# Projections of keys and queries: full rows in four matmuls against half rows in eight pairs

## Chip, cores and metric

The kernel runs on one core of one Trainium2 chip. The metric is the device time of one execution in microseconds; the time of a kernel is the median of its runs. The times before are 278.46, 279.36, 278.23 and 278.74 us, median 278.6 us.

## What is computed

The reference is a linear attention with an exponential feature map, followed by a gated MLP that mixes along the sequence. There are 8 batches, 8 heads, 576 tokens and head size 64; the feature map has 128 features, the MLP 512 inputs and 2 x 512 hidden units.

```
def phi(x):
    proj = einsum('bhsd,df->bhsf', x, w_phi)            # 64 -> 128
    proj = proj - max(abs(proj), axis=-1)
    return concatenate([exp(proj), exp(-proj)], axis=-1)
q_p, k_p = phi(q), phi(k)
kv = einsum('bhsf,bhsd->bhfd', k_p, v);  z = sum(k_p, axis=2)
x  = einsum('bhsf,bhfd->bhsd', q_p, kv) / (einsum('bhsf,bhf->bhs', q_p, z) + 1e-6)
h  = relu(x_as[b, s, 512] @ w_in);  u, v = halves of h
v_n = layernorm(v)
out = (u * (w_spatial @ v_n + b_spatial)) @ w_out
```

## The kernel before, in words

**Units.** The attention is cut into 36 units: 32 of them are pairs of heads of one batch over the first 512 tokens, and 4 are the last 64 tokens of two batches and all heads. A unit always has 8 blocks of 128 tokens by 64 features, which lie as `kT` and `qT`, tiles of 128 rows by 4 x 128 columns: in each column block j, rows 0 to 63 are one block and rows 64 to 127 are the next one. For the first two batches TensorE transposes them (`a_transpose`, L248 to L261); for later batches a DMA does (`cross`, L116). The units of the last tokens are always transposed by TensorE, with a copy of `kT` on ScalarE or VectorE and of `qT` on VectorE.

**Projection.** `by_token` (L263) multiplies one half of `kT` or `qT` by `wphi2`, which holds `w_phi` twice on a block diagonal (rows 0 to 63 by columns 0 to 127, rows 64 to 127 by columns 128 to 255, zeros elsewhere). So one matmul with 128 rows and 256 columns projects two blocks at once, half of the products being with zeros. Two such matmuls fill a PSUM bank with 4 blocks; keys take two banks per unit and queries two. For keys (`a_keys`, L270) VectorE takes the maximum of the absolute values over a bank (L278) and ScalarE takes the two exponentials from it (L281); `a_scale` then makes `em` on ScalarE (L301) and the scaled values `vs` on GpSimd (L306). For queries (`a_queries`, L283) VectorE takes the maxima (L292), and GpSimd (VectorE for the first five units) splits them into a bf16 high part and rest, `mhl` (L295, L296). Later steps turn `mhl` by a transpose on TensorE (L327), make the query features (L344 and L365, or L348 to L359), sum keys by values (`a_kv`, L378, L380), and multiply queries by these sums (`a_num`, L398, with reciprocal and product on VectorE, L388, L389).

**Filler.** The MLP of each batch is a list of tasks, mostly groups of 128x512 matmuls of 0.85 to 1.07 us: `b_v` (L447, then ScalarE L449 and VectorE L450, L451; its normalisation on GpSimd, L461 to L467, comes as a task of its own), `b_u` (L515, ScalarE L517), `b_s` (L536, VectorE L539), `b_o` (L561, then VectorE or ScalarE L564 in turn, and a DMA out). They wait in `queue` and are dealt out between the parts of the attention, by a credit in microseconds of matmul time:

```
ORDER = (("keys", 0.375), ("queries", 0.25), ("attention", 0), ("sums", 0.25),
         ("next", 0.125), ("features", 0), ("out", 0), ("maxima", 0))
...
    credit[0] = min(credit[0] + rate[0] * share, CAP)
    while queue and credit[0] >= queue[0][0] / 2:
        cost, task = queue.pop(0)
        task()
        credit[0] -= cost
```

`CAP` is 2.11, and `rate` is at most `MOST` = 4.0 per step (L622 to L637). `step(i)` (L648) runs the parts in the order of `ORDER`, each for the unit that is due by its lag, and calls `fill(share)` after each. What is left of the queue after the last step is run at the end (L737).

**What sets the order.** Each engine runs its instructions in a fixed order, that in which `step` builds them; the framework's scheduler moves only neighbours past each other, and not those under `pin`. So the order of `step` is that of TensorE, VectorE, ScalarE, GpSimd and the DMA queues. All PSUM tiles come from one pool of 8 banks (L57) that are given out in turn: a new tile waits until the tile eight before it has been read.

The profile names lines of this kernel. The first filler task stands in the step of unit 8, and the last projection is that of unit 35.

Of the kernel before, what the change touches and what calls it, by code (L numbers as in the profile page):

```python
# [8 lines left out]
FP32 = mybir.dt.float32  # L9
BF16 = mybir.dt.bfloat16  # L10
AF = mybir.ActivationFunctionType
ALU = mybir.AluOpType
AX = mybir.AxisListType
# [3 lines left out]
def kernel(  # L17
# [15 lines left out]
    nc = tc.nc  # L33

    B, H, S, D = q.shape
    F = w_phi.shape[1]
# [3 lines left out]
    P = 128  # L40
# [16 lines left out]
    psum = ctx.enter_context(tc.tile_pool(name="psum", bufs=8, space=bass.MemoryType.PSUM))  # L57
# [81 lines left out]
    bias = cpool.tile([P, NB], FP32)  # L139
# [8 lines left out]
    wphi2 = cpool.tile([P, 2 * F], BF16)  # L148
# [12 lines left out]
    for i in range(NM):  # L161
        for tiles, name in ((mhl, "mhl"), (mT, "mT")):
            t = cpool.tile([P, P], BF16, name=f"{name}{i}")
# [21 lines left out]
    for y in range(2):  # L185
        r = slice(y * D, (y + 1) * D)
# [7 lines left out]
    for i in range(2):  # L194
        pin(nc.scalar.copy)(out=alternate(wm, i),
                            in_=wphi2[:, i * F:(i + 1) * F].unsqueeze(1).to_broadcast([P, NP, F]))
# [51 lines left out]
    def a_transpose(u):  # L248
        if u["pair"] and u["b"] >= XB:
            return  # L250
        src = st[u["b"]] if u["pair"] else gs[u["g"]]
        for x, copy in (("k", nc.vector.tensor_copy if u["i"] < EK else nc.scalar.copy), ("q", nc.vector.tensor_copy)):
            pt = psum.tile([P, 4, P], BF16, tag="bank", name="pt")
            for j in range(4):
                if u["pair"]:
                    blk = src[x][u["pj"] // 2][:, 2 * (u["pj"] % 2) + j // 2, (j % 2) * P:(j % 2 + 1) * P]
                else:
                    blk = src[x][:, 2 * j:2 * j + 2, :]
                nc.tensor.transpose(out=pt[:, j, :], in_=blk, identity=ident)
            u[x + "T"] = a1.tile([P, 4, P], BF16, tag="kT", name="kT") if x == "k" else qts[u["i"] % len(qts)]  # L260
            copy(out=u[x + "T"], in_=pt)  # L261

    def by_token(xT, half):  # L263
        ps = psum.tile([P, 4, F], FP32, tag="bank", name="ps")
        for x in range(2):
            nc.tensor.matmul(out=ps[:, 2 * x:2 * x + 2, :], lhsT=xT[:, 2 * half + x, :], rhs=wphi2,  # L266
                             start=True, stop=True)
        return ps

    def a_keys(u):  # L270

        u["mk"] = small.tile([P, H], FP32, tag="mk", name="mk")
        u["kf"] = feat.tile([P, 2, H, F], BF16, tag="kf" if u["pair"] else "kf_t", name="kf",
                            bufs=4 if u["pair"] else 2)
        for half in range(2):
            pk = by_token(u["kT"], half)
            hs = slice(4 * half, 4 * half + 4)
            nc.vector.tensor_reduce(out=u["mk"][:, hs], in_=pk, axis=AX.X, op=ALU.max,  # L278
                                    apply_absolute_value=True)
            for s, sc in ((0, 1.0), (1, -1.0)):  # L280
                nc.scalar.activation(out=u["kf"][:, s, hs, :], in_=pk, func=AF.Exp, bias=0.0, scale=sc)  # L281

    def a_queries(u):  # L283

        m, early = mhl[u["i"] % NM], u["i"] < EARLY
        if not early:
            mq = small.tile([P, H], FP32, tag="mq", name="mq")
        for half in range(2):
            pq = by_token(u["qT"], half)
            if early and half == 0:  # L290
                mq = pq[:, 0, 0:H]
            nc.vector.tensor_reduce(out=mq[:, 4 * half:4 * half + 4], in_=pq, axis=AX.X, op=ALU.max,  # L292
                                    apply_absolute_value=True)
        eng = nc.vector if early else nc.gpsimd
        eng.tensor_copy(out=m[:, 0:H], in_=mq)  # L295
        eng.tensor_tensor(out=m[:, H:2 * H], in0=mq, in1=m[:, 0:H], op=ALU.subtract)  # L296

    def a_scale(u):
        em = small.tile([P, 2, H], FP32, tag="em" if u["pair"] else "em_t", name="em", bufs=3 if u["pair"] else 1)
        for s, sc in ((0, -1.0), (1, 1.0)):  # L300
            nc.scalar.activation(out=em[:, s, :], in_=u["mk"], func=AF.Exp, bias=0.0, scale=sc)  # L301
        if u["pair"]:
            pj = u["pj"]
            vs = feat.tile([P, 2, H, DA], BF16, tag="vs", name="vs", bufs=4)
            for s in range(2):
                nc.gpsimd.tensor_tensor(out=vs[:, s, :, 0:D], in0=st[u["b"]]["v"][:, pj * H:(pj + 1) * H, :],  # L306
                                        in1=em[:, s, :].unsqueeze(2).to_broadcast([P, H, D]), op=ALU.mult)
            nc.gpsimd.tensor_copy(out=vs[:, :, :, D:DA], in_=em.unsqueeze(3).to_broadcast([P, 2, H, 2]))
            u["vs"] = vs
        else:  # L310
            d = gs[u["g"]]
            d["vs"], d["unit"], d["em"] = vst[u["g"] % 2], u, em
            for bl in range(2 if u["g"] else 1):
                tail_scale(u["g"], bl)
# [10 lines left out]
    def a_max_t(u):  # L325
        pt = psum.tile([P, P], BF16, tag="bank", name="pt")
        nc.tensor.transpose(out=pt, in_=mhl[u["i"] % NM], identity=ident)  # L327
        if merged(u):
            odd, even = u["qT"][0:2 * H], u["qE"][D:D + 2 * H]
            nc.vector.tensor_copy(out=odd, in_=pt[0:2 * H, :].unsqueeze(1).to_broadcast([2 * H, 4, P]))  # L330
            nc.vector.tensor_copy(out=even, in_=pt[0:2 * H, :].unsqueeze(1).to_broadcast([2 * H, 4, P]))
            return
        nc.vector.tensor_copy(out=mT[u["i"] % NM][0:2 * H, :], in_=pt[0:2 * H, :])
# [34 lines left out]
    def a_kv(u):  # L368
        d, dg, bl = st[u["b"]], gs[u["g"]], u["b"] % 2
        if u["pj"] == 0:  # L370
            d["kv"] = feat.tile([P, H, 2, DA], BF16, tag="kv", name="kv", bufs=3)
        ut = dg["unit"]
        pv = psum.tile([P, 2, 2, DA], FP32, tag="bank", name="pv")
        for hh in range(2):
            h = 2 * u["pj"] + hh
            for s in range(2):
                for c in range(NB):
                    nc.tensor.matmul(out=pv[:, hh, s, :], lhsT=u["kf"][:, s, 4 * hh + c, :],  # L378
                                     rhs=u["vs"][:, s, 4 * hh + c, :], start=(c == 0), stop=False)
                nc.tensor.matmul(out=pv[:, hh, s, :], lhsT=ut["kf"][:, s, h, :],  # L380
                                 rhs=dg["vs"][:, bl, s, h, :], start=False, stop=True)
        copy = nc.vector.tensor_copy if u["i"] < EARLY else nc.scalar.copy
        copy(out=d["kv"][:, 2 * u["pj"]:2 * u["pj"] + 2, :, :], in_=pv)
# [220 lines left out]
    def b_tasks(b):  # L604
# [11 lines left out]
        for y in range(NB):  # L616
# [2 lines left out]
        ts.append((MS / 2, lambda: b_s_tail(g, [bl])))  # L619
        return ts + (out_tasks(b) if b == B - 1 else [])  # L620

    ORDER = (("keys", 0.375), ("queries", 0.25), ("attention", 0), ("sums", 0.25),  # L622
             ("next", 0.125), ("features", 0), ("out", 0), ("maxima", 0))
    MOST = 4.0
    rate = [MOST]
# [15 lines left out]
    def lag(u, what):  # L641
        if u["i"] < 5:
            return (HEAD if u["i"] < 2 else FIRST if u["pair"] else FT).get(what, 0)
        return LAGS.get(what, 0)
# [3 lines left out]
    def step(i):  # L648

        if i == 0:  # L650
            a_transpose(units[0])
        left = [p - i + 1 for p in lists if p >= i]
        rate[0] = min(MOST, sum(cost for cost, _ in queue) / left[0]) if left else MOST
        for what, share in ORDER:
            for u in units[max(0, i - 5):i + 2]:
                if u["i"] + lag(u, what) != i or (what in ("sums", "attention", "out") and not u["pair"]):
                    continue
                last = u["pair"] and u["pj"] == NP - 1
                if what == "keys":
                    a_keys(u)  # L660
                    a_scale(u)
                elif what == "sums":
                    a_kv(u)
                elif what == "queries":
                    a_queries(u)
                elif what == "next":
                    a_transpose(u)
                elif what == "maxima":
                    a_max_t(u)
                elif what == "out":  # L670
                    a_x_t(u)
                    if last:
                        finish_batch(u, tail_x_t)
                        queue.extend(b_tasks(u["b"]))
                elif what == "features":
                    a_qfeat(u)
                elif what == "attention":
                    a_num(u)
                    if last:
                        finish_batch(u, tail_num)  # L680
            fill(share)
# [87 lines left out]
```

## Time and profile before

| | |
|---|---|
| median of 4 runs | 278.6 us |
| the profiled execution: time | 278.46 us |
| the profiled execution: span from first to last instruction | 276.7 us |
| TensorE (PE) busy | 255.4 us, 92% |
| TensorE weight loads (PEld) busy | 172.1 us, 62% |
| VectorE (DVE) busy | 236.5 us, 85% |
| ScalarE (ACT) busy | 218.6 us, 79% |
| GpSimd (POOL) busy | 184.0 us, 67% |
| chain of work that ended last | PE 68%, DVE 10%, ACT 9%, DMA 4%, POOL 3%, issue 3% |
| projection of keys and queries, L266 | 288 matmuls of 128x256, 7% of that chain |

The time of an execution is 1.8 us longer than its span. In a row of the profile, `128*128 128x256 x4` after a MATMUL means four matmuls whose weights have 128 rows by 128 columns and whose moving operand has 128 rows by 256 columns. The length of a matmul's row (some 220 ns for 128 columns) is its whole way through the array; the next one starts much earlier, so the cost of one is read from the distance of starts and not from its length, and "busy" of PE hides short pauses. A weight load has its own row (PEld) and lies beside matmuls.

### The profile page before, as it was taken

What the parts mean: (1) busy time and instruction counts of PE and PEld (TensorE: products, weight loads), DVE (VectorE), ACT (ScalarE), POOL (GpSimd) and SP (SyncE); (2) the same over time, 40 slices, a digit from 0 to 9 for tenths busy, and PEclk for the clock granted to TensorE, in tenths of its full rate; (3) what the DMA queues carried; (4) which work ended last, traced back from release to release, by engine and by line L of the source; (5) the groups of instructions that cost most, each with busy time, mean ns of one, the idle gap of its engine ahead of it and who ended that gap; (6) DMA issues with size and microseconds to landing.
All of it is one profiled execution on the core that took longest, in us unless ns stands there. A gap on an engine that the chain in (4) does not pass through costs nothing.

```text
span 276.7 us, 8138 instructions
## 1 busy us (share of the span) xinstructions
PE 255.4 (92%) x3007; PEld 172.1 (62%) x3047; DVE 236.5 (85%) x614; ACT 218.6 (79%) x501; POOL 184.0 (67%) x312
## 2 busy tenths in 40 slices
PE   3688999999999999999998999999998999999993
PEld 2476876767655676666665776667665765554441
DVE  7989999879999989998989899998898897565751
ACT  7898998797798978999888978998798977633511
POOL 6899899999569954997787954998347632410200
PEclk9979999999999999999999999999999999999999
DMA  7999999999999999999999998999754301211115
GB/s 200 223 236 149 162 144 99 156 232 218 160 196 179 218 218 169 203 181 225 123 118 191 241 206 148 171 227 185 116 94 118 88 2 63 91 41 40 76 40 190
DMA packets 84840, 42.43 MB, mean 153 GB/s; under 512 B 51840, under 2 KB 80192, under 8 KB 84800
## 3 DMA queue, kind: packets, MB, share of 16 engines
q1 hardware_dynamic: 60240, 30.95, 54.2%
q0 software_dynamic: 24400, 10.89, 36.4%
q8 instruction: 24, 0.39, 0.6%
q14 instruction: 16, 0.13, 0.2%
q10 hardware_dynamic: 160, 0.07, 0.1%
HBM read 32.85 MB, written 9.44 MB: 153 GB/s over the span
## 4 chain that ended last, share of the span: by engine, by line
PE 68%; DVE 10%; ACT 9%; DMA 4%; POOL 3%; issue 3%; ACTq 0%; DVEq 0%
PE ps L536 10%; PE pv L447 10%; PE po L561 9%; PE pu L515 8%; PE ps L266 7%; ACT kf L281 5%; PE pv L378 4%; PE pn L398 4%; PE pq L344 3%; DVE mk L278 3%; PE ps L537 2%; POOL vs L306 2%; DMA q_bf<-in_q_dram 2%; DMA v_tl<-in_v_dram 2%; PE pn L426 2%
## 5 line engine op out<-in xcount | busy, mean ns | idle before, releaser
L306 POOL TENSOR_TENSOR vs<-v_f,em 128x512 bf16<-128x512 f32 x64 | 65.5, 1043 | 27.3 <-ACT em L301 24.8
L281 ACT ACTIVATE kf<-ps 128x512 bf16<-128x512 f32 x144 | 75.3, 633 | 6.6 <-DVE mk L278 6.5
L365 ACT ACTIVATE qf<-pq 128x512 bf16<-128x512 f32 x128 | 66.5, 620 | 9.8 <-PE pq L344 7.5
L278 DVE TENSOR_REDUCE mk<-ps 128x4 f32<-128x512 f32 x72 | 46.3, 681 | 1.1 <-PE ps L266 0.5
L292 DVE TENSOR_REDUCE mq<-ps 128x4 f32<-128x512 f32 x62 | 39.9, 678 | 2.1 <-PE ps L266 2.0
L561 PE MATMUL po<-w_out_bf,uT 128*128 128x512 bf16 x120 | 31.9, 379 | 1.4 <-ACT kf L281 0.8
L461 POOL TENSOR_TENSOR rs<-var,neghalf 64x1 f32<-64x1 f32 (+1 forms) x16 | 12.8, 799 | 30.4 <-DVE var L456 30.2
L536 PE MATMUL ps<-w_spT,vn 128*128 128x512 bf16 x119 | 32.5, 379 | 0.5
L450 DVE BATCH_NORM_STATS2 stats<-vr 128x6 f32<-128x512 bf16 (+1 forms) x40 | 26.7, 684 | 6.5 <-ACT vr L449 6.2
L447 PE MATMUL pv<-w_in_bf,xT 128*128 128x512 bf16 x117 | 30.7, 379 | 1.3 <-ACT kf L281 0.6
L515 PE MATMUL pu<-xT,w_in_bf 128*128 128x512 bf16 x119 | 31.1, 379 | 0.5 <-issue 0.2
L449 ACT ACTIVATE vr<-pv 128x512 bf16<-128x512 f32 (+1 forms) x40 | 23.8, 618 | 8.8 <-PE pv L447 8.1
L539 DVE TENSOR_TENSOR uT<-ps,uT 128x512 bf16<-128x512 f32 x32 | 22.0, 687 | 8.5 <-PE ps L537 7.6
L378 PE MATMUL pv<-vs,kf 128*128 128x66 bf16 x512 | 24.5, 193 | 1.3 <-ACT kf L281 1.2
L389 DVE TENSOR_TENSOR x<-pn,rc 128x256 bf16<-128x256 f32 x64 | 25.0, 416 | 0.3
L398 PEld LDWEIGHTS <-qf 128*128 128x128 bf16 x512 | 20.2, 97 | 7.4 <-issue 1.7
L517 ACT ACTIVATE uT<-pu 128x512 bf16<-128x512 f32 x32 | 19.6, 639 | 6.3 <-PE pu L515 3.2
L378 PEld LDWEIGHTS <-kf 128*128 128x128 bf16 x512 | 21.7, 97 | 2.8 <-issue 2.0
L398 PE MATMUL pn<-kv,qf 128*128 128x66 bf16 x512 | 21.9, 193 | 0.9 <-ACT kf L281 0.3
L564 ACT COPY ob<-po 128x512 f32<-128x512 f32 x18 | 11.0, 611 | 14.3 <-PE po L561 8.8
L467 POOL TENSOR_SCALAR vn<-vr,rs 128x512 bf16<-128x512 bf16 x28 | 21.3, 769 | 0.9
L380 PE MATMUL pv<-vst,kf 128*128 128x66 bf16 x128 | 21.2, 191 | 0.5 <-POOL vst L61 0.5
(130 smaller groups left out, 563.8 us busy)
## 6 DMA issues: line engine op xcount, KB each, us to landing
out_dram<-ob SPq DMA_DIRECT2D x32, 256.0 KB, 2.8
v_f<-in_v_dram SPq DMA_DIRECT2D x14, 512.0 KB, 6.2
k_bf<-in_k_dram POOLq DMA_DIRECT2D x14, 256.0 KB, 5.9
q_bf<-in_q_dram POOLq DMA_DIRECT2D x14, 256.0 KB, 6.0
qt<-qT_b SPq DMA_DIRECT2D x24, 64.0 KB, 4.1
v_tl<-in_v_dram SPq DMA_DIRECT2D x8, 128.0 KB, 5.8
v_f<-in_v_dram SPq DMA_DIRECT2D x1, 1024.0 KB, 8.6
w_in_bf<-in_moe_w_in_dram POOLq DMA_DIRECT2D x2, 512.0 KB, 5.8
```

Source lines behind the costliest of these rows:

```text
L278: nc.vector.tensor_reduce(out=u["mk"][:, hs], in_=pk, axis=AX.X, op=ALU.max, apply_absolute_value=True)
L281: nc.scalar.activation(out=u["kf"][:, s, hs, :], in_=pk, func=AF.Exp, bias=0.0, scale=sc)
L292: nc.vector.tensor_reduce(out=mq[:, 4 * half:4 * half + 4], in_=pq, axis=AX.X, op=ALU.max, apply_absolute_value=True)
L306: nc.gpsimd.tensor_tensor(out=vs[:, s, :, 0:D], in0=st[u["b"]]["v"][:, pj * H:(pj + 1) * H, :], in1=em[:, s, :].unsqueeze(2).to_broadcast( ...
L365: nc.scalar.activation(out=qf[:, s], in_=pq, func=AF.Exp, bias=0.0, scale=sc)
L378: nc.tensor.matmul(out=pv[:, hh, s, :], lhsT=u["kf"][:, s, 4 * hh + c, :], rhs=u["vs"][:, s, 4 * hh + c, :], start=(c == 0), stop=False)
L398: nc.tensor.matmul(out=pn[:, pos, :], lhsT=u["qf"][hh][:, s, pos, :], rhs=d["kv"][:, 2 * u["pj"] + hh, s, :], start=(s == 0), stop=(s == 1))
L447: nc.tensor.matmul(out=pv[r], lhsT=lhs(kc), rhs=w_in_bf[:, kc, HALF:DFF], start=(kc == 0), stop=(kc == KC - 1))
L450: nc.vector.bn_stats(out=stats[r], in_=dst[r])
L515: nc.tensor.matmul(out=pu, lhsT=w_in_bf[:, kc, dc * P:(dc + 1) * P], rhs=d["xT"][:, kc, :], start=(kc == 0), stop=(kc == KC - 1))
L536: nc.tensor.matmul(out=ps, lhsT=d["vn"][:, sp, cs], rhs=w_spT[:, sp, 0:T0], start=(sp == 0), stop=False)
L561: nc.tensor.matmul(out=po[r], lhsT=lhs(dc), rhs=w_out_bf[:, dc, :], start=(dc == 0), stop=(dc == KC - 1))
```

## The change

`by_token` now makes both banks of `kT` or `qT` in one call. For each column block it issues two matmuls: one with rows 0 to 63 of `xT` as weights and rows 0 to 63 of `wphi2` as moving operand, into the first bank, and one with rows 64 to 127 of both, into the second bank. Each has 64 rows and 128 columns; the zeros of `wphi2` are no longer used here. A unit has 16 such matmuls, in the place of 8 with 128 rows and 256 columns. The first bank now holds the even blocks and the second the odd ones, so maxima and exponentials are written with a stride (`parity`, and the rearranged outputs of ScalarE, GpSimd and VectorE).

A new `a_project` issues the projections of keys and queries together, at the head of the step, ahead of `a_keys`. The shares of `ORDER` are changed with it: no filler stands between keys and queries any more, and the share of 0.625 follows the queries. The program's output code (`b_o`, `b_o_tail`, `o_mm`) is the same in both kernels, though the description of the change speaks of a last output group in two halves on two queues.

```diff
-    def by_token(xT, half):
-        ps = psum.tile([P, 4, F], FP32, tag="bank", name="ps")
-        for x in range(2):
-            nc.tensor.matmul(out=ps[:, 2 * x:2 * x + 2, :], lhsT=xT[:, 2 * half + x, :], rhs=wphi2,
-                             start=True, stop=True)
+    def by_token(xT):
+        ps = [psum.tile([P, 4, F], FP32, tag="bank", name="ps") for _ in range(2)]
+        for j in range(4):
+            for y in range(2):
+                r = slice(y * D, (y + 1) * D)
+                nc.tensor.matmul(out=ps[y][:, j, :], lhsT=xT[r, j, :], rhs=wphi2[r, y * F:(y + 1) * F],
+                                 start=True, stop=True)
         return ps
+
+    def parity(t, y):
+        return t.rearrange("p (j two) -> p j two", two=2)[:, :, y]
+
+    def a_project(u):
+        u["pk"], u["pq"] = by_token(u["kT"]), by_token(u["qT"])
 
     def a_keys(u):
...
-        for half in range(2):
-            pk = by_token(u["kT"], half)
-            hs = slice(4 * half, 4 * half + 4)
-            nc.vector.tensor_reduce(out=u["mk"][:, hs], in_=pk, axis=AX.X, op=ALU.max,
+        for y, pk in enumerate(u["pk"]):
+            nc.vector.tensor_reduce(out=parity(u["mk"], y), in_=pk, axis=AX.X, op=ALU.max,
                                     apply_absolute_value=True)
             for s, sc in ((0, 1.0), (1, -1.0)):
-                nc.scalar.activation(out=u["kf"][:, s, hs, :], in_=pk, func=AF.Exp, bias=0.0, scale=sc)
+                nc.scalar.activation(out=u["kf"][:, s].rearrange("p (j two) f -> p j two f", two=2)[:, :, y, :],
+                                     in_=pk, func=AF.Exp, bias=0.0, scale=sc)
 
     def a_queries(u):
 
         m, early = mhl[u["i"] % NM], u["i"] < EARLY
-        if not early:
+        if early:
+            mq = u["pq"][0][:, 0, 0:H]
+        else:
             mq = small.tile([P, H], FP32, tag="mq", name="mq")
-        for half in range(2):
-            pq = by_token(u["qT"], half)
-            if early and half == 0:
-                mq = pq[:, 0, 0:H]
-            nc.vector.tensor_reduce(out=mq[:, 4 * half:4 * half + 4], in_=pq, axis=AX.X, op=ALU.max,
-                                    apply_absolute_value=True)
+        for y, pq in enumerate(u["pq"]):
+            nc.vector.tensor_reduce(out=mq[:, 4 * y:4 * y + 4], in_=pq, axis=AX.X, op=ALU.max, apply_absolute_value=True)
         eng = nc.vector if early else nc.gpsimd
-        eng.tensor_copy(out=m[:, 0:H], in_=mq)
-        eng.tensor_tensor(out=m[:, H:2 * H], in0=mq, in1=m[:, 0:H], op=ALU.subtract)
+        hi, lo = (m[:, e * H:(e + 1) * H].rearrange("p (j two) -> p two j", two=2) for e in range(2))
+        mq = mq.rearrange("p (two j) -> p two j", two=2)
+        eng.tensor_copy(out=hi, in_=mq)
+        eng.tensor_tensor(out=lo, in0=mq, in1=hi, op=ALU.subtract)
...
-    ORDER = (("keys", 0.375), ("queries", 0.25), ("attention", 0), ("sums", 0.25),
+    ORDER = (("keys", 0), ("queries", 0.625), ("attention", 0), ("sums", 0.25),
              ("next", 0.125), ("features", 0), ("out", 0), ("maxima", 0))
...
                 if what == "keys":
+                    a_project(u)
                     a_keys(u)
                     a_scale(u)
```

## The prediction, made before the changed kernel ran

> **What bounds the kernel now.** I read the page's busy times first, then the same engines by stage, then the start times of TensorE's matmuls around a change of the array's shape.
>
> The page's totals, and its 40 slices for the two busiest engines:
>
> ```profile
> PE 255.4 (92%) x3007; PEld 172.1 (62%) x3047; DVE 236.5 (85%) x614; ACT 218.6 (79%) x501; POOL 184.0 (67%) x312
> ...
> PE   3688999999999999999998999999998999999993
> ...
> DVE  7989999879999989998989899998898897565751
> ```
>
> PE is full from slice 6 to the end; DVE is nearly full up to slice 32 and then falls away. So there are two regimes. I cut at 40.6 us (the projection of unit 8, with the first filler) and at 220.8 us (that of unit 35). In the windows' table the columns are PE, PEld, DVE, ACT, POOL:
>
> ```profile
> 0.00:40.60 40.60, 30.31 (x417) 24.57 (x418) 37.27 (x108) 35.73 (x83) 34.84 (x57) 0.96 1.02 187
> 40.60:220.80 180.20, 174.22 (x2127) 119.37 (x2160) 163.79 (x418) 156.65 (x368) 138.85 (x238) 1.00 1.12 173
> 220.80:276.70 55.90, 50.87 (x469) 28.13 (x473) 35.47 (x91) 26.19 (x52) 10.34 (x19) 1.00 0.19 67
> ```
>
> The head is DVE's (37.3 of 40.6 us). The last part is PE's alone. In the middle, from the start times in the trace, I added up what exceeds back-to-back distance (216, 109, 56 and 29 ns for 512, 256, 128 and up to 66 columns), leaving out gaps of exactly one missing record and changes of shape: true pauses of PE are 7.9 us in the middle, 12.4 in the head, 0.4 at the end. So PE works 172.3 of 180.2 us in the middle (96%), DVE 163.8 (91%), ACT 156.7 (87%): PE is the bound, with DVE five points behind.
>
> PE's timeline at 105.7 us (start, duration): full-array matmuls, then four with 64 rows (L439), then the full array again:
>
> ```profile
> 105.70 0.28 PE L344 MATMUL pq<-qT_b,wm 128*128 128x128 bf16 x2
> 105.91 0.29 PE L439 MATMUL pt<-ident,xt 64*128 64x64 bf16 x4
> 106.12 0.23 PE L327 MATMUL pt<-ident,mhl 128*128 128x128 bf16 x1
> 106.19 0.60 PE L266 MATMUL ps<-wphi,kT 128*128 128x256 bf16 x4
> 106.63 0.28 PE L548 MATMUL ps<-w_spT,vn 128*128 128x64 bf16 x4
> ```
>
> L266's four take 0.44 us. The two at 105.70 should be over at 105.81, yet L439 starts 0.10 us later; its four (29 ns each) should be over at 106.03, and L327 starts 0.09 later. A visit to the 64-row shape costs 0.19 us.
>
> The only place where half-size tiles stand side by side is eight matmuls with 64-column weights:
>
> ```profile
> 53.18 0.40 PE L236 MATMUL pt<-ident,wsp 128*128 128x128 bf16 x4
> 53.64 0.41 PE L236 MATMUL pt<-ident,wsp 128*64 128x128 bf16 x8
> ```
>
> Eight half tiles last as long as four whole ones. Less the 0.22 us of one matmul's own way, seven distances take 0.19 us: 27 ns each (in the trace 3 to 4 and 52 ns in turn), against 56 ns.
>
> **What the Trainium skill says.** "TensorEngine Tiling (Array Packing)", Key Properties: a change of tiling mode drains TensorE, and different tiles can load weights and multiply in parallel. The trace agrees on both: 0.10 and 0.09 us per change, 27 ns for column tiles. "TensorE: Matmul & The Clock Gate", The mechanism (of row and column tiling): matmuls in different row groups start some 4 ns apart. The trace shows 3 to 4 ns for column tiles; none of its row tiles work in pairs. "PSUM — Partial Sum Buffer", PSUM bank collisions raise a hardware error: two row tiles may not write one bank at once, so the change needs its two banks; no row here bears on that. "TensorEngine Tiling (Array Packing)", PSUM Bottleneck: tiling doesn't speed the reading of PSUM. DVE at 91% is that warning in this trace.
>
> **The change, part by part.**
>
> *Matmuls.* Before, 8 per unit at 109 ns: 0.87 us. After, 16 per unit. In parallel: 16 x 28 = 0.45 us; load plus matmul already runs at 29 ns where a matmul has 64 columns (L548), so loads allow 0.46. One visit to the 64-row shape adds 0.19: 0.65 us. Saved: 0.22 us per unit, 7.9 us over 36. If the pairs don't overlap: 16 x 56 + 190 = 1.09 us, 0.22 us lost per unit. Break-even lies at (0.87 - 0.19)/16 = 42 ns per matmul. I take the parallel value.
>
> *Filler moved.* A step could deal out 4 x (0.375 + 0.25 + 0.25 + 0.125) = 4.0 us. Now 4 x 0.625 = 2.5 is cut to `CAP` 2.11, so at most 3.6. Adding up the filler matmuls (columns / 2400) in both programs' instruction order, from unit 8's projection to unit 35's: 92.5 us before, 87.6 after. So 4.9 us of PE work leave the middle and are run in the last part, where nothing covers them (pauses of 0.4 us): +4.9 us there. Their readers go too: per batch of 16.8 us of filler, DVE does 4.5 x (684 + 168) + 4 x 687 + 2.1 x 674 ns and the small ones, some 8.4 us, and ACT some 7.1. So the middle loses 2.4 us of DVE and 2.1 of ACT.
>
> *Query step moved ahead.* Per unit, two reductions (L292, 0.68 us each) now stand on DVE before the first filler's reader, and POOL's two 0.2 us operations before the filler's normalisation; output DMAs on SP move with their tasks. Reductions and exponentials are as many as before; each filler reader stands up to 1.3 us later and holds its bank longer. Eight banks cover that while PE is not more than a filler task ahead; without the cover PE pauses, which is in the stage sum below.
>
> *Added wait.* The burst needs `qT` and four free banks at the head of the step, with all filler queued behind it on PE. By DMA `qT` has long landed. For the units of last tokens VectorE copies it: at 106.45 to 106.87 us, while the burst's query part would start near 106.4: some 0.4 us. The one at 166 us ended 0.36 us before the burst. At most 1 us in all; I take 0 and keep it in the range.
>
> *Strided writes.* ACT writes four runs of 128 instead of 512 in a row; the nearest row, L529 with strided runs (465 ns for 256), against L383's 400 for 264 dense: between 0 and 0.06 us per instruction. There are 144: 0 to 8.6 us, on an engine with 13% to spare; a gain has no reason. I take 0. Stride in 4 or 8 elements on DVE and POOL: 0 (0.2 us operations, of which a tenth would be 1 us of POOL at 67%).
>
> *Output in two halves.* Not in the diff: 0.
>
> *Sum for the middle.* PE 172.3 - 27 x 0.22 - 4.9 = 161.5; DVE 163.8 - 2.4 = 161.4; ACT 154.6. Now PE and DVE are equally loaded, so what is late next is DVE. With pauses of 7.9 as before the stage takes 169.4; two equal engines wait for each other more, though filler is now even (about 3.4 us a step, before 2.1 to 4.3). I take 3 us more: 172.4, which is DVE at 93.6% (up to 98% in single 20 us stretches of this trace). Middle -7.8, last part +4.9 - 0.2 (unit 35), head 0: it is DVE's, and PE pauses there anyway; 1.0 at best. Net -3.1 on the profiled 278.46 us, which is 0.1 us off the median: **275.4 us**.
>
> **Rivals.**
> 1. *All of PE's saving arrives* (0.14). Pauses stay at 7.9: middle -10.8, +4.7, head up to -1.0: 271.4 to 272.4, say 271.9. For it: even filler. Against: DVE would stand at 95% over 170 us.
> 2. *DVE takes the stage* (0.16). The middle shrinks by only 2 to 5 us while the 4.9 moved to the end are paid in full: 278.2 to 281.2, say 279.5. It decides if the middle exceeds 175.5 us, DVE under 92%. For it: bursts of four reductions (2.6 us) with readers behind them.
> 3. *Row tiles don't overlap* (0.09), the slower one. Place: the 16 matmuls of every burst; price 0.22 us per unit; it decides above 42 ns a matmul. Middle: PE 172.3 + 5.9 - 4.9 + 7.9 = 181.2 (+1.0), last part +5.1: 284.6. Against it: L236's pairs, which however are column tiles.
> 4. *Something outside these* (0.03): the burst's waits or strides eat everything, near 278.5.
>
> **How the numbers follow.** The likeliest case has 0.57 and its own range of 273 to 277.6 (pauses from 0.6 to 5.2 us longer than before). Faster by over 0.3% (0.8 us, about what measurement tells from no change): 0.57 + 0.14 = 0.71. Rival 2 splits about evenly, so same 0.08 + 0.03 = 0.11, and slower 0.08 + 0.09, with rounding 0.18. The range leaves out rival 3, half of rival 1 and the ends of 2 and 4: 271.8 to 280.3.
>
> **What would show it.** Right: starts of the half-row matmuls alternate between a few ns and some 52; a burst and its two changes of shape take about 0.65 us; unit 35's projection starts near 213 us and about 60.5 us of span follow it; DVE is busy 93 to 94% in the middle. Wrong: distances of 56 ns throughout (rival 3); the middle at 176 us or more with PE waiting for reductions or exponentials (rival 2); L281's successor clearly over 640 ns (strides).

## The result, and the profile after

The changed kernel takes 280.27 us (median of 34 runs) against 278.83 us of the kernel before on the same chips: ratio 1.0061, 95% interval 1.0047 to 1.0075. It is slower by 0.6%, where 1.1% faster was forecast (275.4 us against 278.6 us). The profiled execution took 281.4 us with a span of 279.6 us, 1.1 us above the median of its kernel; that of the kernel before is 0.4 us below its own. So of the 2.9 us between the two traces 1.5 us are spread between executions. Executions more than 1.5% above the fastest of their kernel are left out of the ratios below; the profiled one of e15 is such, so its stages are not given.

The page of the changed kernel, busy times, the slices of PE and DVE, and the chain of work that ended last by engine:

```profile
PE 252.9 (90%) x3294; PEld 164.4 (59%) x3335; DVE 236.0 (84%) x614; ACT 218.2 (78%) x501; POOL 185.4 (66%) x312
...
PE   3688899999998999989998999899998899999993
...
DVE  6978999979999889997989899997999957835751
...
PE 44%; DVE 26%; ACT 17%; issue 6%; POOL 3%; DMA 2%; SPq 0%; POOLq 0%; DVEq 0%; ACTq 0%
```

TensorE works less, and the chain tells where it went: PE's share of it was 68% and is 44%, DVE's was 10% and is 26%, ACT's 9% and 17%. The windows of the changed kernel, cut at the projections of units 8 and 35 as before (columns PE, PEld, DVE, ACT, POOL):

```profile
0.00:42.40 42.40, 31.33 (x481) 24.50 (x481) 37.56 (x108) 35.61 (x83) 35.76 (x57) 1.00 0.98 179
42.40:217.50 175.10, 165.18 (x2304) 109.03 (x2336) 161.04 (x412) 153.75 (x362) 134.98 (x232) 1.00 1.15 174
217.50:279.60 62.10, 56.42 (x512) 30.86 (x518) 37.35 (x97) 28.85 (x58) 14.62 (x25) 0.99 0.21 71
```

The middle is 5.1 us shorter (180.2 before), the last part 6.2 us longer (55.9), the head 1.8 us longer (40.6). I added up PE's pauses from the start times, again without missing records and changes of shape, but now only those of over 40 ns: in the middle 6.3 us before (7.9 in the prediction, which had no such floor) and 11.4 us after. What remains of the middle, PE's work, is 173.9 us before and 163.7 after. So the matmul time did go, by 10.2 us, and half of that came back as pauses.

Sorted by place, some 2.1 of the 6.3 us stand before, in or right after projections of keys and queries, and 5.3 of the 11.4 us do. That is 3.2 of the 5.1 us of growth. The rest of the growth lies mostly at the key sums, where TensorE waits for the key exponentials of ScalarE, 2.7 us in the whole span against 1.2 before:

```profile
L378 PE MATMUL pv<-vs,kf 128*128 128x66 bf16 x512 | 24.5, 193 | 1.3 <-ACT kf L281 1.2
...
L385 PE MATMUL pv<-vs,kf 128*128 128x66 bf16 x512 | 25.0, 195 | 2.7 <-ACT kf L287 2.7
```

TensorE at one burst, the changed kernel and then the kernel before at the same place of the program:

```profile
119.93 0.22 PE L334 MATMUL pt<-ident,mhl 128*128 128x128 bf16 x1
120.08 0.40 PE L268 MATMUL ps<-wphi,kT_b 64*128 64x128 bf16 x8
120.31 0.39 PE L268 MATMUL ps<-wphi,qT_b 64*128 64x128 bf16 x8
121.57 0.38 PE L522 MATMUL pu<-xT,w_in_bf 128*128 128x512 bf16 x1 [0.87 <-DVE ob L571]
```

```profile
119.72 0.22 PE L327 MATMUL pt<-ident,mhl 128*128 128x128 bf16 x1
119.77 0.60 PE L266 MATMUL ps<-wphi,kT_b 128*128 128x256 bf16 x4
120.21 1.03 PE L561 MATMUL po<-w_out_bf,uT 128*128 128x512 bf16 x4
121.07 1.03 PE L515 MATMUL pu<-xT,w_in_bf 128*128 128x512 bf16 x4
```

Eight half-row matmuls take 0.23 us (120.08 to 120.31), 28 to 29 ns each, and the trace mostly shows starts 3 to 4 and 52 to 53 ns apart in turn: row tiles do run side by side. The burst is over at some 120.6 us. Then TensorE stands for 0.96 us, waiting for an output copy (L571) on VectorE. In the kernel before there is no pause at this place. The reason at this place is in the bank count. Query features (2 banks), maxima (1) and burst (4) take seven banks within 1.2 us; the filler after them needs the bank of the filler *before* them. VectorE, changed kernel:

```profile
119.40 1.46 DVE L457 BATCH_NORM_STATS2 stats<-vr 128x6 f32<-128x512 bf16 x2
120.78 0.16 DVE L458 BATCH_NORM_AGGREGATE mv<-stats 128x2 f32<-128x6 f32 x1
120.86 0.66 DVE L571 COPY ob<-po 128x512 f32<-128x512 f32 x1
```

The copy that frees this bank stands behind two statistics of filler tasks and ends at 121.52 us; L522 starts at 121.57. Before, two filler tasks stood between the keys' and the queries' matmuls, so TensorE asked for that bank later. The same wait stands at 178.5 us of the changed kernel (1.08 us, again for L571).

### The profile page after: what moved, and what is told of

Its sections match the earlier page's. It is cut to its first block, busy times and chain, and to the rows that moved or that the text cites. A ratio compares the mean times of both kernels' runs of the same rounds, so it can differ in the third digit from the quotient of the medians.

```text
span 279.6 us, 8714 instructions
## 1 busy us (share of the span) xinstructions
PE 252.9 (90%) x3294; PEld 164.4 (59%) x3335; DVE 236.0 (84%) x614; ACT 218.2 (78%) x501; POOL 185.4 (66%) x312
## 4 chain that ended last, share of the span: by engine, by line
PE 44%; DVE 26%; ACT 17%; issue 6%; POOL 3%; DMA 2%; SPq 0%; POOLq 0%; DVEq 0%; ACTq 0%
ACT kf L287 10%; PE ps L543 8%; PE pu L522 6%; PE po L568 6%; DVE mk L284 5%; DVE stats L457 5%; PE pv L454 4%; PE pv L385 3%; ACT qf L372 3%; PE ps L268 2%; PE pn L405 2%; DVE mq L298 2%; PE ps L544 2%; DVE x L396 2%; ACT vr L456 2%
## 5 line engine op out<-in xcount | busy, mean ns | idle before, releaser
L287 ACT ACTIVATE kf<-ps 128x512 bf16<-128x512 f32 x144 | 75.1, 624 | 9.2 <-DVE mk L284 9.0
L298 DVE TENSOR_REDUCE mq<-ps 128x4 f32<-128x512 f32 x62 | 39.5, 678 | 0.0
L522 PE MATMUL pu<-xT,w_in_bf 128*128 128x512 bf16 x123 | 31.3, 379 | 1.2 <-DVE ob L571 0.9
L302 POOL CAST mhl<-mq 128x8 bf16<-128x8 f32 x31 | 5.9, 190 | 29.7 <-DVE mq L298 29.6
L571 ACT COPY ob<-po 128x512 f32<-128x512 f32 x18 | 10.8, 601 | 15.6 <-issue 10.9
```

The costliest lines, as they stand in the source:

```text
L287: nc.scalar.activation(out=u["kf"][:, s].rearrange("p (j two) f -> p j two f", two=2)[:, :, y, :], in_=pk, func=AF.Exp, bias=0.0, scale=sc)
L298: nc.vector.tensor_reduce(out=mq[:, 4 * y:4 * y + 4], in_=pq, axis=AX.X, op=ALU.max, apply_absolute_value=True)
L522: nc.tensor.matmul(out=pu, lhsT=w_in_bf[:, kc, dc * P:(dc + 1) * P], rhs=d["xT"][:, kc, :], start=(kc == 0), stop=(kc == KC - 1))
```

## The experiments

All ratios are to the kernel before on the same chip, with the 95% interval. "Pauses" and "work" are those of PE in the middle, from the profiled execution, counted as above; work is the stage less the pauses. Each stage is read from one execution, so differences of a few tenths of a us in these columns mean nothing. The runs with relieved readers change the output and are probes only.

| run | rows, order | ratio (interval) | middle | pauses | work |
|---|---|---|---|---|---|
| before | full, two places | 1 | 180.2 | 6.3 | 173.9 |
| after | half, burst, share cut | 1.0061 (1.0047 to 1.0075) | 175.1 | 11.4 | 163.7 |
| e4 | full, burst, share cut | 1.0070 (1.0054 to 1.0087) | 176.0 | 7.0 | 169.0 |
| e1 | half, burst, share not cut | 0.9996 (0.9977 to 1.0015) | 180.7 | 12.6 | 168.1 |
| e2 | half, burst, old shares | 0.9994 (0.9978 to 1.0009) | 180.9 | 12.4 | 168.5 |
| e3 | half, two places | 1.0020 (1.0003 to 1.0038) | 180.9 | 7.5 | 173.4 |
| e5 | e2, VectorE relieved | 0.9921 (0.9895 to 0.9947) | 179.7 | 10.9 | 168.8 |
| e6 | before, VectorE relieved | 0.9880 (0.9863 to 0.9896) | 178.1 | 4.5 | 173.6 |
| e8 | e2, work from DVE to PE | 0.9993 (0.9975 to 1.0011) | 178.7 | 5.7 | 173.0 |
| e9 | before, work from DVE to PE | 1.0046 (1.0031 to 1.0060) | 180.5 | 2.1 | 178.4 |
| e10 | e2, early loads | 0.9980 (0.9956 to 1.0004) | 180.1 | 11.5 | 168.6 |
| e11 | e2, DVE and ACT relieved | 0.9846 (0.9813 to 0.9880) | 176.6 | 7.3 | 169.3 |
| e12 | before, DVE and ACT relieved | 0.9861 (0.9838 to 0.9883) | 176.8 | 3.0 | 173.8 |
| e13 | half, burst, spread | 0.9885 (0.9858 to 0.9911) | 178.1 | 9.3 | 168.8 |
| e14 | full, two places, spread | 0.9967 (0.9948 to 0.9985) | 180.2 | 6.5 | 173.7 |
| e16 | e13, early loads | 0.9908 (0.9874 to 0.9941) | 177.3 | 8.5 | 168.8 |
| e17 | full, burst, spread | 0.9933 (0.9907 to 0.9959) | 179.0 | 5.1 | 173.9 |
| e15 | e13, DVE and ACT relieved | 0.9735 (0.9688 to 0.9781) | | | |
| e18 | e16, DVE and ACT relieved | 0.9733 (0.9701 to 0.9765) | 176.3 | (a) | (a) |
| e19 | full, burst, spread, early loads, DVE and ACT relieved | 0.9818 (0.9805 to 0.9831) | 176.7 | 2.9 | 173.8 |

(a) e18's middle holds a stretch at half the clock (last section), which this count can't part from pauses.

The first theory was that the filler pushed to the end is the loss (A in the expectations), and that the middle's pace is set by the engines that read PSUM (VectorE, ScalarE), so that saved matmul time turns into waiting (B); the rival was that the burst itself makes TensorE wait (C, D and E).

**The parts of the change alone.**

e1, the ceiling raised:

```diff
-    CAP = 2.11
+    CAP = 3.11
```

> The changed kernel with the credit's ceiling CAP raised from 2.11 to 3.11, so that the share of 0.625 is dealt out in full; the filler ahead of unit 35 is 92.5 us again, as in the kernel before, in place of 87.6. Theory A (filler pushed to the end): the middle is held by latencies and readers and not by matmuls, so the filler fits back into its pauses and the last part is 4.9 us shorter: about 276 us. Theory B (readers, VectorE above all, hold the middle in proportion to their load): the filler brings back its 2.4 us of VectorE work, the middle grows by about 3 us and more, total about 278 us. Theory C (the burst itself makes TensorE wait for banks and readers): more filler right after the burst makes it worse, 280 us or more.

e2, the shares of the kernel before, with the burst kept:

```diff
-    ORDER = (("keys", 0), ("queries", 0.625), ("attention", 0), ("sums", 0.25),
+    ORDER = (("keys", 0.375), ("queries", 0.25), ("attention", 0), ("sums", 0.25),
```

> The changed kernel with the shares of the kernel before (0.375 after the keys, 0.25 after the queries): matmuls of keys and queries still in one burst of half rows, but the filler and its readers stand again between the maxima of keys and those of queries. Filler ahead of unit 35: 92.5 us. Theory A: as with the raised ceiling, about 276 us. Theory B: about 278 us. Theory C: the query banks are now held over the fillers' readers too, so 280 us or more.

e3, half rows at two places (e2 without the common burst):

```diff
-                    a_project(u)
...
-        for y, pk in enumerate(u["pk"]):
+        for y, pk in enumerate(by_token(u["kT"])):
...
+        two = by_token(u["qT"])
...
-        for y, pq in enumerate(u["pq"]):
+        for y, pq in enumerate(two):
```

> Half rows alone: keys and queries projected apart, at their places of the kernel before, with its shares. TensorE changes its shape four times per unit: 0.46 + 0.38 = 0.84 us per unit against 0.87 before, so hardly any matmul time is saved. Theories A and B: as before, 278.5 us within 1 us. Theory C: as before too, or 1 us better, and then better than the changed kernel because the burst is gone.

e4, the kernel before with the burst and the shares of the changed one (full rows):

```diff
+                    u["pk"], u["pq"] = [[by_token(u[x], h) for h in range(2)] for x in ("kT", "qT")]
                     a_keys(u)
...
-            pk = by_token(u["kT"], half)
+            pk = u["pk"][half]
...
-            pq = by_token(u["qT"], half)
+            pq = u["pq"][half]
...
-    ORDER = (("keys", 0.375), ("queries", 0.25), ("attention", 0), ("sums", 0.25),
+    ORDER = (("keys", 0), ("queries", 0.625), ("attention", 0), ("sums", 0.25),
```

> The burst and the new shares alone, with the full-row matmuls of the kernel before (0.87 us per unit). Filler ahead of unit 35: 87.6 us. Theory A: the 4.9 us at the end are paid, and the middle gains those same 4.9 us only as far as matmuls hold it: 279 to 281 us. Theory B: the same, 280 us. Theory C: the burst's waits come on top of a full TensorE: 282 us or more.

Dealing out the whole share, in either way, takes the loss away: from 1.0061 to 0.9996 and 0.9994. So the share cut by `CAP` costs the changed kernel 0.65%. Theory A's 276 us was missed in both (278.96 and 278.59 us; B had 278). What is left of half rows and burst together is nothing (0.9994), and half rows at equal order (after against e4) are worth 0.1%, inside the intervals. The windows of e4, and the middle of e2:

```profile
40.60:216.60 176.00, 169.96 (x2091) 116.10 (x2122) 161.09 (x411) 153.91 (x362) 134.88 (x232) 1.00 1.12 173
216.60:278.80 62.20, 56.52 (x505) 30.90 (x510) 37.48 (x98) 28.97 (x58) 14.66 (x26) 1.00 0.21 71
...
39.50:220.40 180.90, 170.71 (x2341) 111.38 (x2373) 163.28 (x417) 156.96 (x368) 138.92 (x238) 1.00 1.15 172
```

TensorE works 5.3 us more in this middle than in the changed kernel's (169.0 against 163.7), and the stage is only 0.9 us longer. In e2 the middle is as long as before (180.9) with 5.4 us less work and 6.1 us more pauses. e3 shows the other price: two visits to the 64-row shape per unit use the saving up (work 173.4), and the run is no faster than before.

**Are the readers the bound?** e5 and e6 shorten the query maxima, in the half-row kernel and in the kernel before:

```diff
-            nc.vector.tensor_reduce(out=mq[:, 4 * y:4 * y + 4], in_=pq, axis=AX.X, op=ALU.max, apply_absolute_value=True)
+            nc.vector.tensor_reduce(out=mq[:, 4 * y:4 * y + 4], in_=pq[:, :, 0:F // 2], axis=AX.X, op=ALU.max, apply_absolute_value=True)
```

> Half rows in one burst with the shares of the kernel before, and less work on VectorE: the maxima of the queries are taken over 64 of the 128 features only (this changes the maxima, and so the output). That takes some 17 us of VectorE work out of the middle (163.3 to about 146); TensorE has 164 us of work there, ScalarE 157. Theory B (the middle's 181 us are set by the readers, VectorE first, and TensorE only waits for them): the middle falls to 168 to 173 us, the total to 267 to 271 us. Rival D (TensorE is held by the burst's own waits for banks and operands, not by the readers' load): the middle stays above 177, the total above 275 us.

> The kernel before with the same cut in VectorE's work (query maxima over 64 of 128 features, which changes the output). TensorE's 172.3 us of work in the middle are as before. Theory B: TensorE now is the bound, the middle falls only to 175 to 178 us and the total to 273 to 276 us, 4 us or more behind the half-row kernel with the same cut: there the saved matmul time comes out at last. Rival D: no more than 1 us between the two.

e8 and e9 move work from VectorE to TensorE:

```diff
-        return u["pair"] and u["b"] >= XB
+        return u["pair"] and u["b"] >= XB and u["pj"] % 2 == 0
```

> Half rows in one burst with the shares of the kernel before, and work moved from VectorE to TensorE: every second unit of the later batches takes its maxima by four matmuls with a selector and one copy (the way of the first two batches) in place of two copies of 16x512. For 12 units VectorE does 0.6 us less each (7 us), TensorE 0.43 us more (5 us), which is about what the half rows save. Same output. Theory B: the middle falls by 5 us or more, the total to 272 to 275 us, faster than both kernels. Rival D: no gain, 278 us.

> The same move of work from VectorE to TensorE in the kernel before, which has no matmul time to give: TensorE 177 us of work in the middle, VectorE 157. Theory B: TensorE becomes the bound, the middle stays at 180 to 183 us, the total at 278 to 281 us. Rival D: the same.

Theory B fell with e5: 12 us less of VectorE's work in the middle (151.2 against 163.3 in e2; 17 had been counted on) took 0.7% off the half-row kernel, where it should have taken 3 to 4%, and did not put it ahead of the full-row kernel with the same relief (0.9921 against 0.9880). e6 came out at 275.69 us, within 1 us of e5, as D had it. e8 gained nothing, but against e9 it shows that saved matmul time is worth something once TensorE has more to do: 0.9993 against 1.0046, intervals apart.

**The burst's own waits.** In e2's profile the largest single pause was this, TensorE at unit 10:

```profile
53.83 0.40 PE L268 MATMUL ps<-wphi,kT_b 64*128 64x128 bf16 x8
55.50 0.40 PE L268 MATMUL ps<-wphi,qT_b 64*128 64x128 bf16 x8 [1.27 <-DMA qT_b<-q_bf]
```

The burst asks for the queries some 1.4 us before the DMA transpose has landed; all filler stands behind it. e10 loads them earlier:

```diff
-    at(7, load, "k", 2, 0)
-    at(7, load, "q", 2, 0)
-    at(8, load, "k", 2, 1)
-    at(8, load, "q", 2, 1)
+    at(6, load, "k", 2, 0)
+    at(6, load, "q", 2, 0)
+    at(7, load, "k", 2, 1)
+    at(7, load, "q", 2, 1)
```

> Half rows in one burst with the shares of the kernel before, and the keys and queries of the third batch loaded one step earlier. In the run without this, TensorE stood for 1.46 us inside the burst of unit 10, at 54 us, until the DMA transpose of its queries had landed; the query projection has been moved ahead by the burst. Theory E (TensorE's saving is taken by waits of the burst itself, for operands that are not there yet and for banks): that wait goes, total 1.0 to 1.8 us less, 277.0 to 277.7 us. Theory B (readers set the pace, a wait that is taken away comes back later): no change, 278.6 us.

e13 deals the filler out in four equal shares, one of them between the feature matmuls and the burst (the diff is against e2):

```diff
-    ORDER = (("keys", 0.375), ("queries", 0.25), ("attention", 0), ("sums", 0.25),
-             ("next", 0.125), ("features", 0), ("out", 0), ("maxima", 0))
+    ORDER = (("keys", 0.25), ("queries", 0.25), ("attention", 0), ("sums", 0.25),
+             ("next", 0), ("features", 0), ("out", 0), ("maxima", 0.25))
```

> Half rows in one burst with the filler dealt out in four equal shares of 0.25: after the keys, after the queries, after the sums, and after the maxima, that is between the feature matmuls and the burst, where none stood before. As much filler ahead of unit 35 as in the kernel before. Features, maxima and burst together take seven banks within 1.2 us; now a filler task of 0.9 us stands among them. Theory E: the pauses inside and right after the burst (about 5 us in the middle) fall by half, total 276 to 277.5 us. Theory B: no change, 278.6 us.

e11 and e12 relieve both readers: the query maxima as in e5, and of the key exponentials `((0, 1.0), (1, -1.0))[:2 - y]`, with the sums reading the first one where the second is missing.

> Half rows in one burst with the shares of the kernel before, and both readers relieved: query maxima over 64 of 128 features (VectorE 17 us less), and for half of the key blocks the second exponential is left out, the sums reading the first one in its place (ScalarE 23 us less); both change the output. VectorE then has about 148 us of work in the middle, ScalarE 140, TensorE 169 with its changes of shape. Theory B: with the readers out of the way the stage comes down to TensorE's work, total 266 to 270 us. Theory E: the burst's waits for operands and banks stay in part, total 270 to 275 us.

> The kernel before with both readers relieved in the same way (output changed). TensorE has 174 us of work in the middle with its changes of shape. Theory B: TensorE alone is the bound, total 272 to 274 us, 4 us or more behind the half-row kernel with the same relief. Theory E: 272 to 274 us too, and within 2 us of the half-row kernel.

e13 is 275.4 us, 0.9885: faster than both kernels, and below e2 by 1.1%. e10 alone is not told apart from no change, though in its profile the wait of 1.4 us at unit 10 is down to 0.6 us in four pieces. The pauses at the projections are 3.5 us in e13, against 5.8 us in e2. TensorE in e13, at the burst of the fence above:

```profile
119.41 0.22 PE L334 MATMUL pt<-ident,mhl 128*128 128x128 bf16 x1
119.46 1.03 PE L522 MATMUL pu<-xT,w_in_bf 128*128 128x512 bf16 x4
120.42 0.40 PE L268 MATMUL ps<-wphi,kT_b 64*128 64x128 bf16 x8
121.04 0.40 PE L268 MATMUL ps<-wphi,qT_b 64*128 64x128 bf16 x8 [0.22 <-DVE ob L571]
121.68 1.02 PE L568 MATMUL po<-w_out_bf,uT 128*128 128x512 bf16 x4 [0.24 <-DVE x L396]
```

The one pause of 0.96 us has become two, 0.41 and 0.33 us. Relieved readers (e11, e12) again leave half rows and full rows within 0.15% of each other. e11 took 274.4 us, where theory B had 266 to 270; in its middle PE works 4.5 us less than in e12 and pauses 4.3 us more, of which 3 us stand at the burst. So with both readers relieved the saving still went into pauses there.

**Is it the half rows, or the spread?** Controls: e14 is the kernel before with e13's `ORDER`; e17 is e4 with it; e15 is e11 with it; e16 is e13 with the loads of e10; e18 adds e10's loads to e15, and e19 is e17 with those loads and the same relief.

> The control for the spread filler: the kernel before (full rows, keys and queries apart) with the same four shares of 0.25. Theory E (half rows save matmul time, which the burst's want of banks took away and the spread gives back): without half rows and burst the spread gives little, 278 to 280 us, 2.5 us or more behind the half-row kernel with it. Rival F (the spread alone is the gain, half rows and burst do nothing): 275 to 276 us, the same as the half-row kernel with it.

> Full rows in one burst with the four shares of 0.25. Theory E: TensorE works 5.5 us more in the middle than with half rows, so 279 to 281 us, some 4 us or more behind the half-row kernel with the spread. Rival F: 275 to 277 us.

> Half rows in one burst, filler spread in four shares of 0.25, and both readers relieved (query maxima over 64 of 128 features; half of the key blocks without their second exponential, which changes the output). Theory E: banks and readers both out of the way, TensorE's 169 us of work in the middle come out, 269 to 272 us, against 274.4 without the spread and 274.8 of the full-row kernel with relieved readers. Rival F: 271 us too, so this run alone doesn't tell them apart; it shows what is left beside.

> Half rows in one burst, filler spread in four shares of 0.25, and the third batch's keys and queries loaded one step earlier. In the spread kernel's profile TensorE stood 0.76 us in the burst of unit 10 for the landing of its queries. Theory E: 0.5 to 1 us less than the spread alone, 274.4 to 275 us. Theory B: no difference.

> Half rows in one burst, filler spread in four shares of 0.25, the third batch loaded one step earlier, both readers relieved as before (query maxima over half of the features, half of the key blocks without their second exponential; output changed). Theory E+B (what takes the saving are waits for banks and for the readers that free them): with both eased, half rows are ahead of full rows by most of the 5.3 us that TensorE works less: 270 to 272 us. Rival G (something else, such as the DMA transposes, sets the middle's pace): no more than 1.5 us ahead.

> The same with full rows in the burst: banks, loads and readers eased, and TensorE with 174 us of work in the middle. Theory E+B: TensorE is the bound, 274 to 276 us, 3 us or more behind half rows. Rival G: within 1.5 us of half rows.

Neither theory got it whole. E's forecast for e17 was missed (279 to 281 us; it took 276.48, as F had it), and that of F for e14 too (275 to 276; it took 277.61). Of e13's 1.15%, the spread alone gives 0.33% (e14); spread and burst with full rows give 0.67% (e17). The 0.25 to 0.5% that half rows seem to add (e16 and e13 against e17) is not shown, as the intervals overlap. With early loads and relieved readers as well, half rows are ahead by 0.85% (e18 against e19, intervals apart). That is 2.4 us of the 5 us or so that TensorE works less in the middle (168.8 us in e13, 173.9 in e17); "most of the 5.3 us" was forecast. e16 shows no gain over e13. e18's profiled execution, 2.3 us above the median of its kernel, has one long pause, for a transfer of the attention's output:

```profile
107.00 0.81 PE L454 MATMUL pv<-w_in_bf,xT 128*128 128x512 bf16 x3
110.14 0.39 PE L454 MATMUL pv<-w_in_bf,xT 128*128 128x512 bf16 x1 [2.33 <-DMA xT<-x]
```

e19 waits 0.90 us at the same place. Whether e18's other executions wait as long is not known; the 2.3 us above the median suggest that most don't.

## Why the prediction was wrong, point by point

- *Matmuls: right.* Row tiles overlap, 28 ns each; a change of shape into the burst costs 152 - 56 = 96 ns, and one out of it 148 - 52 = 96 ns where nothing waits. PE's work in the middle fell by 10.2 us (5.9 + 4.9 = 10.8 was forecast).
- *The step that failed: "two equal engines wait for each other more ... I take 3 us more", in the sum for the middle.* With this term the forecast still credited half rows and burst with 3.1 us (27 x 0.22 + 0.2 - 3). With all filler dealt out they give almost nothing: e2 is at 0.9994, that is 0.2 us, and e1 at 0.9996. The profile of e2 has work -5.4, pauses +6.1, middle +0.7. So the waits cost twice what was allowed, and all of the half rows' gain went into them. In the changed kernel pauses grew by 5.1 us and the middle shrank by 5.1 and not by 7.8; that shrinking is what the filler left behind (e4's middle shrank by 4.2 us with full rows).
- *A second step that failed: filler moved, booked as -4.9 us in the middle and +4.9 us at the end, so at nothing.* The amount was right, but the move costs 0.65%, or 1.8 us (after against e1 and e2). The last part grew by 6.2 us where 4.7 was forecast; it has pauses of some 1.1 us at the burst of unit 35 and the sums after it. With the 2.9 us of the step above, this makes up the whole miss of 4.8 us (1.1% faster forecast, 0.6% slower measured).
- *The cover that I named was not there.* "Eight banks cover that while PE is not more than a filler task ahead" was wrong for the burst: features, maxima and burst take seven banks in a row, so the next filler depends on a reader that was queued just before. And "By DMA `qT` has long landed" was wrong at unit 10 of e2, where the burst stood 1.4 us for it; in the changed kernel, which comes there 2.4 us later, it stood 0.3 us. The wait for VectorE's copy of a last-token unit, taken as 0 of at most 1 us, was 0.45 us at 48.9 us.
- *Rival 2 came nearest.* It had 278.2 to 281.2 us, and a stage that no longer follows TensorE; the middle, 175.1 us, stopped just short of its line of 175.5. Its reason was VectorE's load, and e5 and e11 speak against load alone.
- *Head: 0 forecast, +1.8 us in the profiled execution.* This can't be put down to the change. VectorE, ScalarE and GpSimd run the same instructions in the same order in the heads of the changed kernel, e1, e2 and e13, and these take 42.4, 41.5, 39.5 and 41.4 us, so from 1.1 us under the 40.6 of the kernel before to 1.8 over it. In the changed kernel's trace the first cast of GpSimd ends a wait for a load at 7.03 us and not at 6.18.
- *Strided writes: right.* L287 takes 624 ns in the mean, L281 took 633 before (means of the groups on the two pages).

Not settled: how the 5 us or so that went into waits divide among banks, readers and landings. Each eased alone gave half rows no lead over full rows (e5 against e6, e11 against e12) or no clear gain (e10); eased together they gave 0.85% of the whole (e18 against e19). That banks run short at the burst is seen in the trace at two places, and the spread took some 2 us off the pauses there. That banks are the main part was not shown, as the spread helps the full-row kernels too, and it evens the shares besides putting filler ahead of the burst. Full rows in one burst with the old shares, the direct counterpart of e2, was not run.

## What to carry to other kernels

An engine that works 96% of a stage is not thereby the stage's only bound: before crediting a saving on it, count for each moved instruction what it asks for (operands, banks) at its new place and who frees that, eight tiles back in a pool of eight. Work that is gathered into a burst to save a change of shape takes away the distance that hid its readers; here it helped to put other work in front of the burst, not only behind it (e13 against e2, 1.1%). And when shares of a dealt-out budget are merged, look for a ceiling that cuts the sum.

## What was not expected of the hardware

Pairs of 64-row matmuls with 128 columns reach the full factor of two (28 ns against 56 ns) although each has its own weight load, whose row in the trace is 94 ns long. A change between the 128-row and the 64-row shape costs some 0.095 us in each direction. For a burst of 16 the two take 0.19 us, nearly half of the 0.45 us that side-by-side tiles save. In e18, after the standstill at 107 us, the granted clock fell for a while: it was 0.50 from 112 to 114 us, and pairs of the burst at 112.6 us start 107 ns apart there, twice the usual 56.
